# Down-sampled attention: 112 keys by head plus 32 keys by query group in place of 80 and 64

## The chip, the cores and the metric

The kernel runs on one core of a Trainium2 chip, in one launch. The metric is the device time of that core in microseconds. Three runs of the kernel before took 971.51, 972.09 and 972.30 us, a median of 972.09 us.

## What is computed

An attention layer over 8 batches, 8 heads, 576 positions and 64 values per head is followed by a two-layer feed-forward block over 4608 tokens. The attention is the sum of two parts: one on means of four positions, repeated four times, and one in a band of width 7.

```python
q_d, k_d, v_d = (mean over 4 positions of q, k, v)      # 144 positions
out_d = softmax(q_d @ k_d.T / 8) @ v_d
out_up = np.repeat(out_d, 4, axis=2)
mask = np.abs(pos[:, None] - pos[None, :]) < 4
out_local = softmax(where(mask, q @ k.T / 8, -1e9)) @ v
x = (out_up + out_local), heads side by side            # 4608 x 512
h = x @ w_in                                            # 4608 x 2048
out = (s * np.maximum(h, 0) ** 2 + b) @ w_out           # 4608 x 512
```

The change touches the product `softmax(...) @ v_d` alone.

## The kernel before

**Feed-forward.** Tokens are cut into 18 tiles of 256 (t), the 2048 hidden columns into 8 parts of 256 (p). A step (t, p) is `gemm1` (24 matmuls `ph`, lines 556 to 558, 256 columns each) and, two or three steps later, `gemm2` (12 matmuls `po`, lines 601 to 603, 512 columns each). Each operand is split into a high and a low part in a reduced format, which is why every product stands there three times.

**Attention.** A pair is one batch and two heads; there are 32. The first 12 pairs go through `first_unit`, which does the band on TensorE too: `sl` (line 388, scores, in tiles of 64 rows by 32 columns of the array) and `ol` (line 431, 128 rows by 64 columns, so that a matmul of one head writes the upper 64 output partitions and that of the other head the lower). The other 20 pairs go through `two_pairs`, two at a time: `down_unit` for each of the two pairs, and beside it `local_unit`, which does the band on VectorE and GpSimd (`pr`, `st`, `pv`, `acc`, lines 466 to 488).

**The down-sampled part, `down`.** All 32 pairs go through it. Two query groups of both heads lie in one matrix: `qc` is block diagonal, so that one matmul `sa` (line 303) gives for query group i (48 queries, 3 groups) the scores of both heads in 96 output partitions, with 144 key columns. The exponentials `pd` are scaled on ScalarE (line 314). Then they have to be transposed, since the next product sums over keys. The 144 keys are cut in KM = 80 and KR = 64:

- three transposes `tp` (lines 322, 325) put the first 80 keys of each query group in 80 partitions, and three `tr` (line 327) the last 64 keys in 64 partitions;
- ScalarE copies `tp` to `ptm` (line 329) and `tr` to `ptr` (line 332), the two heads' 64 keys one above the other;
- GpSimd adds the four positions of each value: lines 287 and 288 make two partial sums `vt`, `vq` out of the loaded `tvd`, `tvr`, and lines 291 and 292 write them into `vm` (each head's 64 columns, zeros in the other 64) and into the block-diagonal `vdr`;
- `up` (lines 337, 339) is then three matmuls that all use the whole array: 128 rows by 128 columns for the 64 keys of both heads, and twice 80 rows by 128 columns, once for each head. In the trace a float32 matmul is two records, so `up` is six of them, `sa` six, and a transpose one.

`vm` and `vdr` lie in a constant tile `dq` for all pairs but three, so GpSimd writes them for the next pair only when `up` of this one is done.

**What orders the work.** The program is recorded in the order of the step loop, and `advance` draws so many pieces of attention per step from a generator by numbers of due steps. Then a scheduler orders each engine's queue by a simulation of its own, with priorities: `first(b)` gives `sa`, `tp`, `tr` and `up` of batches 3 to 7 a high one, so that they stand wherever the simulation has them ready, also between two `ph` or `po`. Every engine then runs its queue strictly in that order. All loads go through SyncE's one queue (SP).

## Time and profile before

| what | value |
|---|---|
| median of 3 runs | 972.09 us |
| the profiled execution itself | 972.49 us |
| its span | 970.7 us |
| TensorE (PE) busy | 938.7 us, 97% of the span |
| TensorE weight loads (PEld) | 843.4 us, 87% |
| VectorE (DVE) busy | 637.7 us, 66% |
| ScalarE (ACT) busy | 475.0 us, 49% |
| GpSimd (POOL) busy | 418.0 us, 43% |

The span is the time from the first to the last recorded instruction; 1.8 us of the execution lie around it. In the timeline a row has the start, the duration, engine, line, operation, output and inputs, then rows by columns of the weights, the result's shape, and the count of merged records. Matmuls are pipelined: a row's duration runs from the entry of the first column to the exit of the last, so that rows overlap, and the price of a matmul in a stream is the distance from its start to the next start, not its duration.

### The profile page before, as it was taken

Reading aid. Unit: us, or ns where it says so; the run is one execution under the profiler, and the core shown is the slowest. Engines: PE = TensorE matmul, PEld = TensorE weight load, DVE = VectorE, ACT = ScalarE, POOL = GpSimd, SP = SyncE. Lnnn points to the kernel's source line nnn. Section 1 sums busy time; section 2 is a strip of 40 time slices with the busy share of each in tenths; the row PEclk is TensorE's granted clock in tenths of the full one; section 3 lists DMA queues with packets and bytes.
Section 4 is the critical chain, followed back from the end, with each engine's and each line's share of the span. In section 5 each row is a group of like instructions: output and inputs, shape, how many; then the busy total and the mean of one; then the engine's idle time right before and its main releaser. Section 6 shows DMA issues by size and latency. Waiting matters only on the chain.

```text
span 970.7 us, 18541 instructions
## 1 busy us (share of the span) xinstructions
PE 938.7 (97%) x7316; PEld 843.4 (87%) x7316; DVE 637.7 (66%) x1175; ACT 475.0 (49%) x1141; POOL 418.0 (43%) x455
## 2 busy tenths in 40 slices
PE   5769999999999999999999999999999999999998
PEld 4559988888999999998888899989899999998987
DVE  5999996864567878787787878787878521211121
ACT  5878775553754453545363545453635433333231
POOL 9421011101066686776868786867676200000000
PEclk9999999999999999999999999999999999999999
DMA  9736512112243232323241424242412000000000
GB/s 316 261 121 210 172 60 78 49 42 73 101 134 113 77 110 72 102 70 133 67 136 66 135 68 131 72 134 69 136 55 76 1 22 1 23 1 22 1 23 22
DMA packets 32103, 86.26 MB, mean 89 GB/s; under 512 B 3344, under 2 KB 7952, under 8 KB 32016
## 3 DMA queue, kind: packets, MB, share of 16 engines
q1 hardware_dynamic: 32016, 85.08, 26.6%
q8 instruction: 57, 0.93, 0.4%
q14 instruction: 30, 0.25, 0.1%
HBM read 75.63 MB, written 9.44 MB: 88 GB/s over the span
## 4 chain that ended last, share of the span: by engine, by line
PE 74%; DVE 9%; DMA 8%; POOL 5%; ACT 2%; issue 2%; SPq 0%; DVEq 0%; ACTq 0%; POOLq 0%
PE ph L556 11%; PE ph L557 11%; PE ph L558 11%; PE po L603 11%; PE po L601 11%; PE po L602 11%; DMA tqk<-in_qk_dram 3%; POOL pr L466 3%; POOL acc L488 3%; DMA wst<-in_moe_w_out_dram 2%; PE sa L303 2%; DVE bias L579 1%; PE up L339 1%; PE ol L431 1%; DMA lqk<-in_qkn_dram 1%
## 5 line engine op out<-in xcount | busy, mean ns | idle before, releaser
L556 PE MATMUL ph<-xh,wi 128*128 128x256 f32 x1152 | 325.4, 283 | 3.7 <-ACT xh L542 2.5
L557 PE MATMUL ph<-xl,wi 128*128 128x256 f32 x1152 | 323.9, 281 | 0.0
L558 PE MATMUL ph<-xh,wi 128*128 128x256 f32 x1152 | 323.6, 281 | 0.0
L466 POOL TENSOR_TENSOR pr<-lqk 128x576 f32<-128x576 f32 x140 | 201.2, 1461 | 73.2 <-DMA lqk<-in_qkn_dram 29.2
L556 PEld LDWEIGHTS ph<-xh,wi 128*128 128x128 f32 x1152 | 217.5, 189 | 11.2 <-ACT xh L542 2.8
L557 PEld LDWEIGHTS ph<-xl,wi 128*128 128x128 f32 x1152 | 217.4, 189 | 5.4 <-issue 0.2
L558 PEld LDWEIGHTS ph<-xh,wi 128*128 128x128 f32 x1152 | 217.6, 189 | 0.3
L566 ACT ACTIVATE ph<-ph 128x512 f32<-128x512 f32 x144 | 83.8, 582 | 229.0 <-PE ph L558 223.2
L601 PE MATMUL po<-wo,gh 128*128 128x512 f32 x456 | 180.7, 396 | 0.0
L602 PE MATMUL po<-wo,gh 128*128 128x512 f32 x456 | 180.5, 396 | 0.0
L603 PE MATMUL po<-wo,gl 128*128 128x512 f32 x456 | 177.9, 397 | 0.0
L569 DVE TENSOR_TENSOR gl<-ph,gh 128x512 fp32r<-128x512 f32 x114 | 77.8, 683 | 115.8 <-ACT gh L568 115.5
L488 POOL TENSOR_TENSOR acc<-acc,pv 128x576 f32<-128x576 f32 x80 | 114.4, 1430 | 57.1 <-DVE acc L488 29.5
L468 DVE TENSOR_REDUCE st<-pr 128x9 f32<-128x576 f32 x140 | 105.9, 757 | 37.7 <-POOL pr L466 35.4
L292 POOL TENSOR_TENSOR dq<-vq 64x64 f32<-64x64 f32 x58 | 22.8, 393 | 197.4 <-PE up L337 195.3
L603 PEld LDWEIGHTS po<-wo,gl 128*128 128x128 f32 x456 | 85.7, 188 | 17.6 <-issue 0.2
L487 DVE TENSOR_TENSOR pv<-lv,st 128x576 f32<-128x576 f32 x120 | 87.5, 747 | 18.8 <-POOL acc L488 18.4
L601 PEld LDWEIGHTS po<-wo,gh 128*128 128x128 f32 x456 | 85.7, 188 | 15.9 <-ACT gh L568 0.6
L602 PEld LDWEIGHTS po<-wo,gh 128*128 128x128 f32 x456 | 85.7, 188 | 15.8
L568 ACT CAST gh<-ph 128x512 fp32r<-128x512 f32 x114 | 66.9, 587 | 64.3 <-PE po L602 62.4
L567 ACT ACTIVATE ph<-ph 128x512 f32<-128x512 f32 x144 | 83.7, 582 | 3.2
L602 PE MATMUL po<-wo,gb 128*128 128x512 f32 x120 | 47.1, 392 | 0.0
(149 smaller groups left out, 1239.3 us busy)
## 6 DMA issues: line engine op xcount, KB each, us to landing
tqk<-in_qk_dram SPq DMA_DIRECT2D x30, 584.0 KB, 4.1
lqk<-in_qkn_dram SPq DMA_DIRECT2D x20, 768.0 KB, 4.2
lv<-in_vn_dram SPq DMA_DIRECT2D x20, 480.0 KB, 3.4
out_dram<-os SPq DMA_DIRECT2D x17, 512.0 KB, 3.1
wst<-in_moe_w_in_dram SPq DMA_DIRECT2D x7, 1024.0 KB, 6.5
wst<-in_moe_w_out_dram SPq DMA_DIRECT2D x7, 1024.0 KB, 5.3
tvd<-in_vdm_dram SPq DMA_DIRECT2D x29, 160.0 KB, 2.9
tvr<-in_vr_dram SPq DMA_DIRECT2D x29, 128.0 KB, 3.1
```

What stands on the lines that cost most here:

```text
L466: nc.gpsimd.tensor_tensor(pr, lqk[:, 0:CH], lqk[:, CH + o : 2 * CH + o], ALU.mult)
L468: nc.vector.tensor_reduce(ls[:, :, o], pr, AX.X, ALU.add)
L487: nc.vector.tensor_tensor(pv, lv[:, o : o + CH], w, ALU.mult)
L488: (nc.vector if o % 3 == 1 else nc.gpsimd).tensor_tensor(acc[:, :, h], acc[:, :, h], pv, ALU.add)
L556: nc.tensor.matmul(ph[:, j], wi[p][:, 0, k, f], xh[:, k], start=(k == 0), stop=False)
L557: nc.tensor.matmul(ph[:, j], wi[p][:, 0, k, f], xl[:, k], start=False, stop=False)
L558: nc.tensor.matmul(ph[:, j], wi[p][:, 1, k, f], xh[:, k], start=False, stop=(k == NK - 1))
L566: nc.scalar.activation(ph, ph, AF.Relu)
L567: nc.scalar.activation(ph, ph, AF.Square)
L601: nc.tensor.matmul(po[m], gh[:, j, ms], wo[p][:, 0, j], start=first, stop=False)
L602: nc.tensor.matmul(po[m], gh[:, j, ms], wo[p][:, 1, j], start=False, stop=False)
L603: nc.tensor.matmul(po[m], gl[:, j, ms], wo[p][:, 0, j], start=False, stop=last)
```

## The change

KM goes from 80 to 112 and KR from 64 to 32.

- **Last keys.** The last 32 keys of the three query groups are no longer scaled in place: VectorE writes them, scaled, side by side in a tile `rest` (96 queries by 3 times 32 keys). One transpose `tr` puts them in 96 partitions, 32 for each query group. Three copies instead of two put them in `ptr`, which is block diagonal over query groups and zero elsewhere (it took the room of `vdr` and `vm` in `dq`). The values of the last 32 keys are loaded three times, one below the other.
- **First keys.** Three transposes `tp` have 112 key columns instead of 80.
- **Sums of values.** Two additions each for `tvd` and `tvr`, in place, in the tile that the DMA filled. `vt`, `vq`, `vm` and `vdr` are gone, and the matmuls read `tvd` and `tvr` themselves.
- **`up`.** Four matmuls instead of three. Each is 64 columns wide and writes the 64 output partitions of one head: two with 112 rows (`tvd`, `ptm`), then two with 96 rows (`tvr`, `ptr`).
- Loads grow by 64 KB each for `tvd` and `tvr`, per pair.

```diff
-KM = 80
+KM = 112
 KR = SD - KM
+NR = NQ * KR
...
-        vt = tmp([P, 2, P], "vt")
-        vq = tmp([P, 2, D], "vq")
-        ve = nc.gpsimd
-        ve.tensor_tensor(vt[0:KM], tvd[:, 0:2], tvd[:, 2:4], ALU.add)
-        ve.tensor_tensor(vq, tvr[:, 0:2], tvr[:, 2:4], ALU.add)
-        for h in range(2):
-            hs = slice(64 * h, 64 * h + 64)
-            ve.tensor_tensor(vm[:, h, hs], vt[0:KM, 0, hs], vt[0:KM, 1, hs], ALU.add)
-            ve.tensor_tensor(vdr[hs, hs], vq[hs, 0], vq[hs, 1], ALU.add)
+        for v in (tvd, tvr):
+            nc.gpsimd.tensor_tensor(v[:, 0:2], v[:, 0:2], v[:, 2:4], ALU.add)
+            nc.gpsimd.tensor_tensor(v[:, 0], v[:, 0], v[:, 1], ALU.add)
...
+        rest = tmp([P, NQ, KR], "rest")[0:n]
+        nc.vector.tensor_tensor(
+            rest, pd[:, :, KM:SD], dsm.unsqueeze(2).to_broadcast([n, NQ, KR]), ALU.mult)
         for i in range(NQ):
-            nc.scalar.mul(pd[:, i], pd[:, i], dsm[:, i : i + 1])
+            nc.scalar.mul(pd[:, i, 0:KM], pd[:, i, 0:KM], dsm[:, i : i + 1])
...
-                for i in range(NQ):
-                    nc.tensor.transpose(tr[:, i], pd[:, i, KM:SD], ident[0:n, 0:n])
+                nc.tensor.transpose(
+                    tr.rearrange("p h q -> p (h q)"), rest.rearrange("p i k -> p (i k)"),
+                    ident[0:n, 0:n])
...
-        for h in range(2):
-            nc.scalar.copy(ptr[64 * h : 64 * h + 64], tr[:, :, GQ * h : GQ * h + GQ])
+        for i in range(NQ):
+            ks = slice(KR * i, KR * i + KR)
+            nc.scalar.copy(ptr[ks, :, GQ * i : GQ * i + GQ], tr[ks])
...
-            nc.tensor.matmul(up, vdr, ptr.rearrange("p i s -> p (i s)"), start=True, stop=False)
-            for h in range(2):
+            for h, hs in heads:
                 nc.tensor.matmul(
-                    up.rearrange("p (i s) -> p i s", i=NQ), vm[:, h],
-                    ptm[:, :, GQ * h : GQ * h + GQ], start=False, stop=h == 1)
+                    up[hs].rearrange("p (i s) -> p i s", i=NQ), tvd[:, 0, hs],
+                    ptm[:, :, GQ * h : GQ * h + GQ], start=True, stop=False)
+            for h, hs in heads:
+                nc.tensor.matmul(up[hs], tvr[:, 0, hs], ptr[:, h], start=False, stop=True)
```

The first place is TensorE's queue where `up` of a group's first pair meets `sa` of its second. Before:

```order
L601 MATMUL po_7805<-wo_1991,gh_8085 128x512
L303 MATMUL sa_8852<-kd_8780,dq_139 96x144 x2
L337 MATMUL up_8774<-ptr_8750,dq_139 128x144
L339 MATMUL up_8774<-ptm_8748,dq_139 128x144
L303 MATMUL sa_8852<-kd_8780,dq_139 96x144
L339 MATMUL up_8774<-ptm_8748,dq_139 128x144
L602 MATMUL po_7805<-wo_1991,gh_8085 128x512
```

The same place in the changed kernel, whose `up` is lines 338 and 342, whose `sa` is line 297 and whose feed-forward lines are one higher:

```order
L604 MATMUL po_8329<-wo_700,gl_8084 128x512
L338 MATMUL up_8692<-ptm_8666,tvd_8411 64x144
L297 MATMUL sa_8767<-kd_8699,dq_139 96x144
L338 MATMUL up_8692<-ptm_8666,tvd_8411 64x144
L297 MATMUL sa_8767<-kd_8699,dq_139 96x144
L342 MATMUL up_8692<-dq_139,tvr_8409 64x144
L297 MATMUL sa_8767<-kd_8699,dq_139 96x144
L342 MATMUL up_8692<-dq_139,tvr_8409 64x144
L602 MATMUL po_8329<-wo_700,gh_8083 128x512
```

The three full-width matmuls of `up`, which stood among those of `sa`, became four half-width ones that alternate with them one by one.

The second place is TensorE's queue in an earlier pair of the changed kernel, where `up` (lines 338 and 342) stands in `ph`:

```order
L558 MATMUL ph<-xl,wi 128x256
L338 MATMUL up<-ptm,tvd 64x144 x2
L559 MATMUL ph<-xh,wi 128x256
L342 MATMUL up<-dq,tvr 64x144 x2
L557 MATMUL ph<-xh,wi 128x256
```

Here the four are in two lots with a `ph` between. Over the 28 pairs whose `up` comes after the first `ph`, the queue of the changed kernel has the four together in 10 pairs, in two lots of two in 8, and one by one in 10. The scheduler also cut other work otherwise: from the first `ph` on, the lots of `sl` and `ol` that stand between full-array matmuls are 29 in the queue before and 37 now, since one `sl` of a late `first_unit` was dealt out one matmul at a time between `ph`.

The third place is the SP queue, in a group late in the program. Before:

```order
L114 DMA tvr_7929<-in_vr_dram 128x256
L114 DMA tvd_7931<-in_vdm_dram 80x512
L461 DMA lv_7322<-in_vn_dram 128x960
L459 DMA lqk_7645<-in_qkn_dram 128x1536
L114 DMA tqk_7927<-in_qk_dram 128x1168
L461 DMA lv_7647<-in_vn_dram 128x960
```

The same place in the changed kernel (`tvd_7250` is read by the second pair of this group, `tvd_7859` by the first of the next):

```order
L460 DMA lqk_7572<-in_qkn_dram 128x1536
L115 DMA tqk_7855<-in_qk_dram 128x1168
L616 DMA out_0_dram<-os_7112 128x2x512
L115 DMA tvd_7250<-in_vdm_dram 112x512
L115 DMA tvr_7248<-in_vr_dram 96x512
L115 DMA tqk_7861<-in_qk_dram 128x1168
L462 DMA lv_7574<-in_vn_dram 128x960
L115 DMA tvd_7859<-in_vdm_dram 112x512
L115 DMA tvr_7857<-in_vr_dram 96x512
L460 DMA lqk_7869<-in_qkn_dram 128x1536
```

The loads of `tvd` and `tvr` were ahead of a group's other loads, and now stand behind the `up` that reads the tile's former content, with `lv` or `lqk` of the band behind them in the queue.

More of the change, by code (lines that the diff above doesn't have):

```diff
@@ L117, in load_pair @@
         tqk = load("qk", [P, 2, SP], qk[b, hp], two)
-        tvr = load("vr", [P, FAC, D], vr_in[b, hp])
+        tvr = load("vr", [NR, FAC, P], vr_in[b, hp])
         tvd = load("vd", [KM, FAC, P], vdm[b, hp])
@@ L174, in attention_ffn_kernel, with blocks @@
     nc.vector.memset(db, 0.0)
[L176 to L181 removed]
+    def blocks(qc, ptr):
+        return take(qc, 0, [P, NQ, 2 * GQ]), take(ptr, 0, [NR, 2, SD])
+    diag = {0: (db, *blocks(dq[:, 0:QC], dq[:, QC:]))}
     def clear(i):
[L184 to L189 removed]
+        da, n = room[i]["dg"], 2 * NG * P
+        ptr = room[i]["sc"][:, 1248:1536]
+        for j in range(0, n + QC, 456):
+            nc.gpsimd.memset(da[:, j : min(j + 456, n + QC)], 0.0)
+        nc.gpsimd.memset(ptr, 0.0)
+        diag[i] = (take(da, 0, [P, 2 * NG, P]), *blocks(da[:, n : n + QC], ptr))
     wi, wo, wst = {}, {}, {}
@@ L268, in down @@
     def down(b, hp, banks, tmp, dg):
-        _, qc, vdr, vm = dg
+        _, qc, ptr = dg
         tqk, _, tvr, tvd = ld[(b, hp)]
@@ L355, in tmp @@
                 return one.tile(shape, F32, tag=name, name=name)
-            if name in ("ups", "ptr"):
-                spots[name] = spots["qd" if name == "ups" else "kd"]
+            if name in ("ups", "ptm"):
+                spots[name] = spots["qd"]
             else:
@@ L407, in first_unit @@
         if own:
-            pt = take(sc, spots["vt"], [P, 2 * NG, 32])
+            pt = tmp([P, 2 * NG, 32], "pt")
         else:
```

23 lines of the change are left out of this document (7 added, 16 removed).

## The prediction

> **What bounds the kernel now.** I read the page's busy times first, then the windows, then the waits, then TensorE's timeline at the places that the change touches. The page, and three stretches of the windows (start and end, length, then busy time of each engine with its instructions, granted clock, DMA share, GB/s):
>
> ```profile
> PE 938.7 (97%) x7316; PEld 843.4 (87%) x7316; DVE 637.7 (66%) x1175; ACT 475.0 (49%) x1141; POOL 418.0 (43%) x455
> ```
>
> ```profile
> 0.00:66.50 66.50, 42.66 (x677) 34.28 (x677) 53.28 (x122) 45.97 (x131) 37.78 (x81) 1.00 0.73 244
> 66.50:275.00 208.50, 206.18 (x2077) 182.35 (x2078) 154.74 (x296) 130.62 (x304) 23.28 (x43) 1.00 0.31 101
> ...
> 550.00:775.00 225.00, 225.00 (x1519) 206.00 (x1518) 179.00 (x324) 108.46 (x275) 159.05 (x151) 1.00 0.27 88
> ```
>
> After the first 66.5 us TensorE has work without a break: 2.3 us idle in the second stretch, none in the third, while VectorE and GpSimd have 46 and 66 us free there. So from 66.5 us on the time is the sum of what stands in TensorE's queue, and an edit is worth what it takes from or adds to that queue. Ahead of that, TensorE waits; the waits show for what:
>
> ```profile
> POOL dq L292 <- PE up L337: 195.3, 13, 33.3
> ...
> PE sa L303 <- DVE kd L278: 7.3, 1, 7.3
> ```
>
> The last row is the longest wait of TensorE: `sa` of the fifth pair, whose q and k come behind the first weights. GpSimd's 195.3 us are waits for `up` before it may write `dq`; nobody on TensorE waits for them.
>
> **The price of `up` and of the transposes.** One `up` between two `ph`:
>
> ```profile
> 760.00 0.28 PE L556 MATMUL ph<-xh,wi 128*128 128x256 f32 x1
> 760.11 0.41 PE L337 MATMUL up<-ptr,dq 128*128 128x144 f32 x2
> 760.36 0.66 PE L339 MATMUL up<-ptm,dq 80*128 80x144 f32 x4
> 760.75 0.38 PE L557 MATMUL ph<-xl,wi 128*128 128x256 f32 x1
> 760.97 0.28 PE L558 MATMUL ph<-xh,wi 128*128 128x256 f32 x1
> 761.09 0.28 PE L556 MATMUL ph<-xh,wi 128*128 128x256 f32 x1
> ```
>
> A `ph` takes 0.12 us (760.97 to 761.09). From 760.00 to 760.97 there are two of them and the six records of `up`: 0.97 - 0.24 = 0.73 us, 0.122 for each pass of 144 columns. The transposes between two `po`:
>
> ```profile
> 756.00 0.25 PE L322 MATMUL tp<-ident,pd 96*80 96x96 f32 x1
> 756.09 0.33 PE L325 MATMUL tp<-ident,pd 96*80 96x96 f32 x2
> 756.25 0.41 PE L327 MATMUL tr<-ident,pd 96*64 96x96 f32 x3
> 756.44 0.48 PE L602 MATMUL po<-wo,gh 128*128 128x512 f32 x1
> 756.76 0.39 PE L603 MATMUL po<-wo,gl 128*128 128x512 f32 x1
> 757.00 0.39 PE L601 MATMUL po<-wo,gh 128*128 128x512 f32 x1
> ```
>
> A `po` takes 0.24, so the six take 756.00 to 756.76 less 0.24, 0.52 us or 0.087 each. `tp` loads 80 columns and `tr` 64, and they take the same: the 96 columns that stream through set the time.
>
> **What half-width matmuls cost.** This trace has them: `ol`, 64 columns wide, one head to the upper and one to the lower output partitions, as the new `up`. Twenty-four records in a row, and twelve:
>
> ```profile
> 268.45 0.28 PE L558 MATMUL ph<-xh,wi 128*128 128x256 f32 x1
> 268.66 1.21 PE L431 MATMUL ol<-db,tvw 128*64 128x96 f32 x24
> 269.80 0.38 PE L556 MATMUL ph<-xh,wi 128*128 128x256 f32 x1
> 270.02 0.28 PE L557 MATMUL ph<-xl,wi 128*128 128x256 f32 x1
> ```
>
> ```profile
> 151.94 0.28 PE L556 MATMUL ph<-xh,wi 128*128 128x256 f32 x1
> 152.15 0.72 PE L431 MATMUL ol<-db,tvw 128*64 128x96 f32 x12
> 152.80 0.38 PE L557 MATMUL ph<-xl,wi 128*128 128x256 f32 x1
> 153.02 0.28 PE L558 MATMUL ph<-xh,wi 128*128 128x256 f32 x1
> ```
>
> With two `ph` taken off, 24 cost 1.57 - 0.24 = 1.33 us and 12 cost 1.08 - 0.24 = 0.84. Twelve more cost 0.49, 0.082 for two, where one full-width pass of 96 columns cost 0.087: the two halves do run side by side. But 0.84 - 0.49 = 0.35 us is left, whatever the number: the price of going into the narrow shape and out again. The smallest lot confirms it, two records of 32 columns in the 64 by 32 shape between single `ph`:
>
> ```profile
> 172.42 0.24 PE L388 MATMUL sl<-tqk 64*32 64x32 f32 x2
> 172.59 0.38 PE L557 MATMUL ph<-xl,wi 128*128 128x256 f32 x1
> 172.91 0.24 PE L388 MATMUL sl<-tqk 64*32 64x32 f32 x2
> ```
>
> One turn takes 0.49; less 0.12 for `ph` and 2 x 0.087/3 = 0.06 for 32 columns twice, 0.31 us stay. Alternating full-width matmuls costs nothing of the kind: `sa` and `up`, mixed,
>
> ```profile
> 694.46 0.65 PE L303 MATMUL sa<-kd,dq 128*96 128x144 f32 x4
> 694.95 0.41 PE L337 MATMUL up<-ptr,dq 128*128 128x144 f32 x2
> ...
> 695.45 0.41 PE L303 MATMUL sa<-kd,dq 128*96 128x144 f32 x2
> ...
> 696.18 0.40 PE L603 MATMUL po<-wo,gl 128*128 128x512 f32 x1
> ```
>
> take 1.72 - 0.24 = 1.48 us for twelve passes, 0.123 each. I take 0.33 us for each lot, with 0.31 and 0.35 as ends.
>
> [...]
>
> **The sum on TensorE**, for the 28 pairs whose `up` comes after the first `ph`, by the lots in the changed queue:
>
> - Four together, 10 pairs: 0.33 + 4 x 0.122 = 0.82 each, 8.2 us.
> - Two lots of two, 8 pairs: each lot holds both heads, 0.33 + 2 x 0.122 = 0.57; 16 lots, 9.1 us.
> - One by one between `sa`, 10 pairs: nothing to share the array with, 0.33 + 2 x 0.122 = 0.57; 40 lots, 22.8 us.
> - Together 40.1 us, for 28 x 0.73 = 20.4 before: +19.7 us.
> - The 37 - 29 = 8 more lots of `sl` and `ol`: 8 x 0.33 = +2.6 us.
> - Transposes, six to four: -2 x 0.087 = -0.17 a pair, -4.8 us. `tp` now loads 112 columns; if loading set the time, 3 x 0.087 x 112/80 + 0.087 x 96/80 = 0.47 for 0.52, -1.4 us. I take -4.8, as 64 and 80 made no difference.
>
> That is +17.5 us. Two rows for the rest:
>
> ```profile
> L287 POOL TENSOR_TENSOR vt<-tvd 80x256 f32<-80x256 f32 x29 | 22.8, 786 | 0.3
> tvd<-in_vdm_dram SPq DMA_DIRECT2D x29, 160.0 KB, 2.9
> ```
>
> **Start.** The first four pairs load 512 KB more ahead of the weights; the fifth pair's `tvr` and `tvd`, 288 KB, move behind its `tqk`. 224 KB at 244 GB/s are 0.9 us on the load that the 7.3 us wait ends with: +1. The five pairs' extra lots fall where TensorE is idle a third of the time. Bounds: -2 (their two transposes and GpSimd's small additions go) to +4 (the lots and their order bind).
>
> **Covered by TensorE's queue.** GpSimd has four additions in place of six, the largest 786 ns as L287's row: no more than before. VectorE gets `rest`, one instruction a pair with 96 numbers a row for the 256 of L287's (an estimate, from another engine's row); ScalarE three short copies for two. All have a fifth or more of their time free after 66.5 us; were that gone, 28 instructions under 0.8 us would be at most 22 us of VectorE. Of the 2.3 us in which TensorE waits now, the longer queue should swallow about 1.
>
> Profiled 972.5 + 17.5 + 1 - 1 = 990.0 us. The profiled execution took 972.49, 0.4 over the median of 972.09, so this stands for the median too.
>
> **Rivals.**
>
> 1. *The lots cost nothing extra*, only the sharing counts. 18 pairs at 0.49 for 0.73 (-4.3), 10 pairs one by one at 0.98 (+2.5), transposes -4.8: 966 us, faster. It decides if a lot costs under 0.08 us. For it is the pairing in `ol`; against it all three rows above. Chance 0.06.
> 2. *One by one between `sa` is cheap*, the price falls once per stretch: 10 x (0.33 + 0.98) = 13.1 for 22.8, 980 us. The `sl` turns at 172 us speak against it. Chance 0.08.
> 3. *`up` doesn't pair*, because the two passes of a head follow each other directly: 0.33 + 0.98 for four, 0.33 + 0.49 for two, 40 x 0.57 one by one, 49.0 for 40.1: 999 us. `ol` stands in the same order of heads and pairs. Chance 0.07.
> 4. *The wait that the change adds.* `tvd` and `tvr` can be loaded only after the `up` of the pair before, SP stands there with `lv` and `lqk` behind it, and GpSimd stands in its own queue until they land (2.9 us, and a little more for the second), with `acc` behind it. `ot` at the end of a group shows the pace:
>
> ```profile
> 676.53 0.98 PE ot L498 x9
> 726.18 0.98 PE ot L498 x9
> ```
>
> 49.65 us a group, to which TensorE's queue now adds 1.55 + 0.09 - 0.34 = 1.3. If GpSimd's chain is as long as TensorE's now and grows by 2.9, it passes it by 1.6 us in 10 groups; half to all of that is 8 to 16 us more, 1002 us. It needs more than 1.3 us of growth. Against it: GpSimd is free 66 of 225 us. Chance 0.12.
>
> The forecast has 0.65. The last 0.02 are for gains and losses that meet near zero.
>
> **Range and chances.** Lots at 0.31 or 0.35 are -1.5 or +1.5 on 74 lots, the transposes up to +3.4, the start -3 to +3: 985 to 998 for the forecast. With rivals 2 and 3 and most of rival 4 inside, 979 to 1004 leaves out rival 1, the near-zero cases and a tail. A difference of 0.2%, 2 us, is about what a measurement of this kernel tells from none. Faster 0.06, within it 0.02, slower 0.92.
>
> **What would show it.** The profile after should have TensorE without a break from about 67 us on; an `up` of four together at about 0.82 us, and one by one with `sa` at about 0.74 + 4 x 0.57 = 3.0 us for 1.48; four transposes at 0.35. I am wrong if those stretches are as short as now, or if TensorE waits for `lv`, `tvd` or `acc` by more than some 4 us after 67 us.

## The result, and the profile after

The changed kernel takes 1006.08 us (median of 4 runs, 1003.33 to 1007.87) beside 971.8 for the kernel before: 1.0353 times as long, 95% interval 1.0326 to 1.038. Slower was right; 990.0 was 16 us too low, and the range ended at 1004. The profiled execution took 1007.87 us, its span is 1006.1. The page's busy times, and the same stretches of the windows:

```profile
PE 965.7 (96%) x7316; PEld 842.6 (84%) x7316; DVE 666.1 (66%) x1207; ACT 476.7 (47%) x1173; POOL 419.1 (42%) x391
```

```profile
66.50:275.00 208.50, 199.25 (x1955) 169.68 (x1954) 152.77 (x292) 120.14 (x282) 22.12 (x28) 0.96 0.31 100
550.00:775.00 225.00, 224.54 (x1458) 197.50 (x1458) 181.05 (x320) 102.89 (x269) 162.27 (x130) 1.00 0.31 96
```

From 550 to 775 us TensorE has next to no break (0.5 us), as forecast. Between 66.5 and 275 us it is idle for 9.3 us (2.3 before), and the granted clock is 0.96. What TensorE waits for in that stretch:

```profile
PE po L602 <- ACT gh L569: 3.8, 3, 2.3
PE sl L384 <- DVE pl L395: 2.5, 1, 2.5
PE sl L384 <- ACT pd L301: 2.2, 1, 2.2
PE ol L432 <- ACT db L415: 0.8, 1, 0.8
```

The clock has to be read with care. The trace of the kernel before has no clock record ahead of 72.6 us, and the windows count a missing record as 1.00; the 1.00 of its first stretch, 0 to 66.5 us, shows nothing. The distance from `ph` to `ph` in that trace shows that it ran at half clock right up to there:

```profile
72.18 0.41 PE L558 MATMUL ph<-xh,wi 128*128 128x256 f32 x1
72.39 0.36 PE L556 MATMUL ph<-xh,wi 128*128 128x256 f32 x1
...
72.83 0.28 PE L556 MATMUL ph<-xh,wi 128*128 128x256 f32 x1
72.95 0.28 PE L557 MATMUL ph<-xl,wi 128*128 128x256 f32 x1
```

0.21 us became 0.12. In the changed kernel `ph` stands 0.21 us apart too where its record has 0.50, up to 67.3 us, and 0.12 behind. The first five `sa` of the kernel before, at 7 to 44 us, take 0.24 us a record as well, for 0.12 behind 72.6. So only what lies behind 72.6 us can be compared. There the kernel before has full clock up to its end. The changed kernel has half clock at 74.1 to 77.5, 173.1 to 179.9, 220.9 to 224.3 and 238.0 to 241.4 us. From 72.6 to 275 us TensorE is idle for 8.1 us (1.8 before), and it is busy for 14.5 us at half clock, of which I count half, 7.3 us, as lost (an estimate, from the recorded 0.50): together some 13.6 us more than before.

**The lots cost what was forecast.** `up` with four passes together between two `ph`, and one by one between `sa`:

```profile
643.49 0.28 PE L559 MATMUL ph<-xh,wi 128*128 128x256 f32 x1
643.70 0.47 PE L338 MATMUL up<-ptm,tvd 112*64 112x144 f32 x4
643.99 0.42 PE L342 MATMUL up<-dq,tvr 96*64 96x144 f32 x4
644.34 0.38 PE L557 MATMUL ph<-xh,wi 128*128 128x256 f32 x1
644.56 0.28 PE L558 MATMUL ph<-xl,wi 128*128 128x256 f32 x1
...
678.93 0.40 PE L604 MATMUL po<-wo,gl 128*128 128x512 f32 x1
679.25 0.46 PE L338 MATMUL up<-ptm,tvd 112*64 112x144 f32 x2
679.64 0.49 PE L297 MATMUL sa<-kd,dq 128*96 128x144 f32 x2
...
681.67 0.46 PE L342 MATMUL up<-dq,tvr 96*64 96x144 f32 x2
682.06 0.50 PE L602 MATMUL po<-wo,gh 128*128 128x512 f32 x1
682.39 0.40 PE L603 MATMUL po<-wo,gh 128*128 128x512 f32 x1
```

643.49 to 644.56 holds two `ph` (0.23) and `up`: 0.84 us, forecast 0.82. 678.93 to 682.39 holds two `po` (0.47) and the mixed stretch: 3.0 us, forecast 3.0; all nine mixed stretches behind 350 us take as long. The transposes:

```profile
586.53 0.25 PE L319 MATMUL tp<-ident,pd 96*112 96x96 f32 x1
586.62 0.33 PE L322 MATMUL tp<-ident,pd 96*112 96x96 f32 x2
586.78 0.25 PE L323 MATMUL tr<-ident,rest 96*96 96x96 f32 x1
586.81 0.48 PE L602 MATMUL po<-wo,gh 128*128 128x512 f32 x1
587.13 0.40 PE L603 MATMUL po<-wo,gh 128*128 128x512 f32 x1
```

587.13 - 586.53 less one `po` is 0.36 us, forecast 0.35: 0.09 each with 112 and 96 columns to load, where 80 and 64 took 0.087.

**Something else is slower: `ph` itself.** The first and the last of the 24 `ph` of one step (t = 15, p = 2), far behind the last attention, before and after:

```profile
839.24 0.28 PE L556 MATMUL ph<-xh,wi 128*128 128x256 f32 x1
...
841.86 0.28 PE L558 MATMUL ph<-xh,wi 128*128 128x256 f32 x1
```

```profile
873.07 0.28 PE L557 MATMUL ph<-xh,wi 128*128 128x256 f32 x1
...
875.82 0.28 PE L559 MATMUL ph<-xh,wi 128*128 128x256 f32 x1
```

23 intervals in 2.62 us (114 ns each) became 2.75 us (119.6). The change does not touch the instructions of `ph`.

**Two stages.** To place a loss I count the 5184 matmuls of `ph` and `po` and take from each trace the start of the 1400th and of the last. The 1400th starts at 331.4 us before and 347.7 after, the last 635.2 us later before and 654.3 after. So 16.3 us are lost in the first stage and 19.1 in the second.

The second stage is what the queue holds: nine mixed stretches at 3.0 for 1.48 us are 13.7 us more, the transposes in it 1.8 us less, and the slower `ph` is 6.4 us (the run with 192 bytes, below). That makes 18.3 of 19.1. In the first stage most of the loss is the idle time and the half clock above.

### The profile page after: what moved, and what is told of

The parts are those of the page before. It is cut to its first block, busy times and chain, and to the rows that moved or that the text cites. A ratio compares the mean times of both kernels' runs of the same rounds, so it can differ in the third digit from the quotient of the medians.

```text
span 1006.1 us, 18578 instructions
## 1 busy us (share of the span) xinstructions
PE 965.7 (96%) x7316; PEld 842.6 (84%) x7316; DVE 666.1 (66%) x1207; ACT 476.7 (47%) x1173; POOL 419.1 (42%) x391
## 4 chain that ended last, share of the span: by engine, by line
PE 81%; DVE 8%; DMA 3%; ACT 3%; POOL 3%; issue 2%; SPq 0%; DVEq 0%; ACTq 0%; POOLq 0%
PE ph L557 13%; PE ph L559 12%; PE ph L558 12%; PE po L602 12%; PE po L603 12%; PE po L604 12%; PE sa L297 2%; DMA tqk<-in_qk_dram 2%; POOL pr L467 2%; PE up L338 1%; PE up L342 1%; POOL acc L489 1%; PE sl L389 1%; PE ol L432 1%; PE ot L499 1%
## 5 line engine op out<-in xcount | busy, mean ns | idle before, releaser
L557 PE MATMUL ph<-xh,wi 128*128 128x256 f32 x1152 | 329.7, 286 | 2.8 <-ACT xh L543 1.4
L559 PE MATMUL ph<-xh,wi 128*128 128x256 f32 x1152 | 326.7, 284 | 0.0
L467 POOL TENSOR_TENSOR pr<-lqk 128x576 f32<-128x576 f32 x140 | 204.3, 1484 | 78.8 <-DMA lqk<-in_qkn_dram 53.3
L557 PEld LDWEIGHTS ph<-xh,wi 128*128 128x128 f32 x1152 | 219.8, 191 | 13.6 <-DVE gl L570 3.1
L558 PEld LDWEIGHTS ph<-xl,wi 128*128 128x128 f32 x1152 | 220.1, 191 | 6.0 <-issue 0.8
L559 PEld LDWEIGHTS ph<-xh,wi 128*128 128x128 f32 x1152 | 219.9, 191 | 1.6 <-issue 1.2
L489 POOL TENSOR_TENSOR acc<-acc,pv 128x576 f32<-128x576 f32 x80 | 116.6, 1457 | 56.8 <-DVE acc L489 40.9
L285 POOL TENSOR_TENSOR tvd<-tvd 112x256 f32<-112x256 f32 x29 | 25.3, 872 | 231.4 <-DMA tvd<-in_vdm_dram 158.2
```

Of the source, the lines that this page charges most:

```text
L467: nc.gpsimd.tensor_tensor(pr, lqk[:, 0:CH], lqk[:, CH + o : 2 * CH + o], ALU.mult)
L489: (nc.vector if o % 3 == 1 else nc.gpsimd).tensor_tensor(acc[:, :, h], acc[:, :, h], pv, ALU.add)
L557: nc.tensor.matmul(ph[:, j], wi[p][:, 0, k, f], xh[:, k], start=(k == 0), stop=False)
L558: nc.tensor.matmul(ph[:, j], wi[p][:, 0, k, f], xl[:, k], start=False, stop=False)
L559: nc.tensor.matmul(ph[:, j], wi[p][:, 1, k, f], xh[:, k], start=False, stop=(k == NK - 1))
```

## The experiments

Each time is a median, and each ratio is to runs of the kernel before on the same chip, with its 95% interval. "First" and "second" are the two stages of the profiled execution.

### Where xh and xl lie

The change makes some tiles smaller and others larger, so everything behind them moves in SBUF. Distances below are from `wi` to `xh` (the same to `xl`) in bytes of one partition. In the kernel before they are 960 for parts 2 to 6 and 320 for parts 0, 1 and 7 (modulo 2048), in the changed kernel 1280 and 320. They follow from the sizes of the tiles; a trace shows no addresses.

```diff
-    split_w(0)
+    gap = one.tile([P, 48], F32, tag="gap", name="gap"); split_w(0)
```

> The changed kernel with 192 unused bytes per partition ahead of wi for parts 0, 1 and 7; every instruction and its order as in the changed kernel. Theory A (the pace of ph is set by how far xh and xl lie from wi in SBUF): the distance for parts 2 to 6 goes from 1280 to 1472 (modulo 2048), which is 192 modulo 256 as it was in the kernel before (960): ph of parts 2 to 6 from 119.7 back to 113.5 ns an interval, 5/8 of 3456 x 6 ns = 12 to 13 us less, 993 to 995 us. Parts 0, 1 and 7 stay at 117.8. Theory B (ph is slower because of what runs beside it, or of the clock): no change, 1006 us.

Measured: 999.89 us, 1.0281 (1.0263 to 1.0299); first 345.4, second 647.9. The same step as above:

```profile
866.00 0.28 PE L557 MATMUL ph<-xh,wi 128*128 128x256 f32 x1
...
868.62 0.28 PE L559 MATMUL ph<-xh,wi 128*128 128x256 f32 x1
```

2.62 us, as in the kernel before. Then the opposite, in the kernel before:

```diff
-    two = ctx.enter_context(tc.tile_pool(name="two", bufs=2))
+    mid = ctx.enter_context(tc.tile_pool(name="mid", bufs=1)); two = ctx.enter_context(tc.tile_pool(name="two", bufs=2))
...
-    sb_s = cst.tile([P, 1], F32, name="sb_s")
+    sb_s = mid.tile([P, 1], F32, name="sb_s")
...
-    sb_b = cst.tile([P, 1], F32, name="sb_b")
+    sb_b = mid.tile([P, 1], F32, name="sb_b")
```

> The kernel before with the two one-number tiles sb_s and sb_b moved behind the weights, so that all of wi lies 64 bytes lower and xh, xl stay; instructions and order as before. Theory A (distance): parts 2 to 6 from 960 to 1024 modulo 2048, the residue 0 modulo 256 that t = 2 has now, 113.5 to 119.7 ns; parts 0, 1 and 7 from 320 to 384, 117.8 to between 118 and 120: +13 to +15 us, 985 to 987 us, without any other part of the change. Theory B (the pace comes from what runs beside): 972 us.

Measured: 979.64 us, 1.0074 (1.0058 to 1.009); first 332.2, second 641.3.

```profile
844.05 0.28 PE L556 MATMUL ph<-xh,wi 128*128 128x256 f32 x1
...
846.80 0.28 PE L558 MATMUL ph<-xh,wi 128*128 128x256 f32 x1
```

Theory A holds both ways, and TensorE's queue has the same order in each pair of kernels; theory B falls. The first edit moves `xh` and `xl` and leaves `wi` of parts 2 to 6 where it was, the second moves `wi` alone: so the pace goes with the distance, not with one operand's place. The size was expected nearly twice as large as it came, because parts 2 to 6 of the kernel before do not run at 113.5 ns throughout: they change between 113.5 and 117.8 from step to step; the mean is 115.3 (here and below, over the intervals from `ph` to `ph` under 130 ns, token tiles from t = 3 on). Behind the 1400th matmul the mean from `ph` to `ph` is 117.9 ns before and 121.1 here, 3.2 x 2372 = 7.6 us.

Last, parts 0, 1 and 7 of the kernel before (`mid` is made as above):

```diff
-                return one.tile(shape, F32, tag=name, name=name)
+                return (mid if name == "ptm" else one).tile(shape, F32, tag=name, name=name)
...
-        lambda shape, name: one.tile(shape, F32, tag=name, name=name),
+        lambda shape, name: (mid if name == "ptm" else one).tile(shape, F32, tag=name, name=name),
```

> The kernel before with ptm's tile moved from ahead of wi for parts 0, 1 and 7 to behind all weights: their distance to xh and xl goes from 320 to 1472 modulo 2048, 192 modulo 256 as parts 2 to 6 have. Theory A (distance): ph of parts 0, 1 and 7 from 117.8 to 113.5 ns, 3/8 of 3456 x 4.3 = 5.6 us at most, half of it if they alternate between the two values as parts 2 to 6 do in the local stage: 966.5 to 969.5 us. Theory B: 972.

Measured: 970.7 us, 0.998 (0.9969 to 0.9991), first 329.9, second 632.3. It is the only kernel here that is faster than the kernel before, by 0.2%. The expectation was mostly missed: those parts went from 117.6 to 116.4 ns in the mean, but parts 2 to 6, whose distance did not change, from 115.3 to 116.2. What these runs show is two classes: at the distances 1280, 1024 and 384, multiples of 128, `ph` took 119.4 to 119.6 ns in the mean; at 960, 320 and 1472, 64 beside a multiple, it took 113.5 or 117.8 in a step and 115.0 to 117.7 in the mean. What chooses between these two stays open, and so does whether the rule is one of 128 bytes.

### The lots of up

In the changed kernel, the operand that is ready last goes first, and `sa` of batches 3 to 7 queues behind the `up` before it:

```diff
+                mm = nc.tensor.matmul(up[hs], tvr[:, 0, hs], ptr[:, h], start=True, stop=False)
...
+                mm = nc.tensor.matmul(
+                    up[hs].rearrange("p (i s) -> p i s", i=NQ), tvd[:, 0, hs],
+                    ptm[:, :, GQ * h : GQ * h + GQ], start=False, stop=True)
+        ups_last[0] = mm
...
+        prev = ups_last[0]
-        with first(b):
+        with first(b), tc.issue_after(getattr(prev, "ins", prev)) if b >= 3 else contextlib.nullcontext():
```

> The changed kernel with the four passes of up always together: tvr with ptr is added first (its operand is ready last), and sa queues behind the up before it. Theory A (each change of shape on TensorE has its price, and only the lots count): 10 stretches with sa from 3.00 to 1.55 us (0.74 + 0.82), -14.5; 8 pairs with two lots from 1.29 to 0.84, -3.6: 988 us. Rival (the time shows up elsewhere: TensorE waits for acc, lv or tvd as long as it was busy with lots): above 1000 us. ph keeps 119.7 ns in parts 2 to 6.

Measured: 1000.71 us, 1.0282 (1.026 to 1.0305); first 346.8, second 651.5. The busy time of TensorE falls by 17 us, to 948.3, and only 5 to 7 us of it arrive: the rival. TensorE now waits in the second stage, 10.2 us from 275 to 800 (2.0 in the changed kernel), the longest first:

```profile
PE ph L560 <- DVE gl L573: 4.0, 4, 1.4
PE po L605 <- ACT gh L572: 2.5, 2, 2.2
PE po L605 <- DVE os L617: 1.0, 2, 0.6
PE tr L325 <- DVE rest L310: 1.0, 2, 0.5
```

No lots for `up` at all:

```diff
-            nc.gpsimd.tensor_tensor(v[:, 0], v[:, 0], v[:, 1], ALU.add)
+            for h in range(2):
+                hs, no = slice(64 * h, 64 * h + 64), slice(64 - 64 * h, 128 - 64 * h)
+                nc.gpsimd.tensor_tensor(v[:, 2 + h, hs], v[:, 0, hs], v[:, 1, hs], ALU.add)
+                nc.gpsimd.memset(v[:, 2 + h, no], 0.0)
...
+                nc.tensor.matmul(up, tvr[:, 2 + h], ptr[:, h], start=h == 0, stop=False)
...
+                    up.rearrange("p (i s) -> p i s", i=NQ), tvd[:, 2 + h],
```

> The changed kernel with up in full columns again: GpSimd puts each head's sums into a slice whose other half it sets to zero, so four passes of 128x128 and no lot for up. Keys stay 112 and 32, four transposes. Theory A (lots): 28 pairs at 4 x 0.122 = 0.49 us against 40.1 us in all as forecast, -26.4 us: 979 to 980 us; what is left over the kernel before is the pace of ph (+12), less the transposes (-4.8). If the stalls and the low clock before 275 us come of the lots of sl and ol too, they go as well: 970 to 972. Rival (GpSimd, with ten short instructions a pair for four, holds up the groups): over 990 us.

Measured: 1001.96 us, 1.0314 (1.0285 to 1.0343); first 349.7, second 645.6. The expectation fails, and the first stage, with no lot of `up` in it, is as long as ever. So taking the lots out is not enough to win it back. This edit also gives GpSimd ten short instructions a pair for four and makes another order, and what these cost was not measured.

And the lots alone, in the kernel before:

```diff
-            nc.tensor.matmul(up, vdr, ptr.rearrange("p i s -> p (i s)"), start=True, stop=False)
...
+            heads = [(h, slice(64 * h, 64 * h + 64)) for h in range(2)]
+            for h, hs in heads:
+                nc.tensor.matmul(
+                    up[hs].rearrange("p (i s) -> p i s", i=NQ), vm[:, h, hs],
+                    ptm[:, :, GQ * h : GQ * h + GQ], start=True, stop=False)
+            for h, hs in heads:
+                nc.tensor.matmul(
+                    up[hs], vdr[:, hs], ptr.rearrange("p i s -> p (i s)"), start=False, stop=True)
```

> The kernel before with up alone in half columns: four passes of 64 columns, one head each, the first keys' pair ahead of the last keys' pair; keys stay 80 and 64, sums, transposes and tiles as before. In TensorE's queue ten pairs have their four passes one by one between sa. Theory A (lots): the ten stretches 1.52 us longer, +15; the other pairs 0.09 each or 0.45 where they are two lots, +2 to +3: 989 us, nearly all of it after the 1400th matmul, ph at the pace of before. Rival (the price needs the changed kernel's other parts): under 980.

Measured: 989.37 us, 1.0181 (1.0164 to 1.0198); first 336.7 (+5.3), second 645.8 (+10.6). Theory A has the total to the microsecond, but it expected nearly all of it behind the 1400th matmul, and a third lies ahead of it. Then together:

```diff
+            for h, hs in heads:
+                mm = nc.tensor.matmul(
+                    up[hs], vdr[:, hs], ptr.rearrange("p i s -> p (i s)"), start=True, stop=False)
...
+        with first(b), tc.issue_after(getattr(prev, "ins", prev)) if b >= 3 else contextlib.nullcontext():
```

> As the run before it, but the four passes always together (the last keys' pair first, sa queued behind the up before). Theory A: 28 lots at 0.33 us with four passes of 0.122 for 0.73 us: +2.5 us in all, later stage +1 to +2. The order in the first stage has the two heads' sl back to back, as in the changed kernel: Theory E adds 3 to 6 us there: 975 to 981 us. If the local chain suffers as it did in the changed kernel with up together (sa behind up): later stage +8 or more, over 982.

Measured: 977.77 us, 1.0058 (1.0043 to 1.0073); first 335.8 (+4.4), second 633.9 (-1.2). Keeping the narrow passes together takes back 11.6 us, the whole loss of the second stage. Here the local chain does not suffer, as it did with the same edit in the changed kernel. So that kernel has something that hinders the chain.

### VectorE's rest

```profile
371.04 1.43 POOL L489 TENSOR_TENSOR acc<-acc,pv 128x576 f32<-128x576 f32 x1
371.65 4.53 DVE L308 TENSOR_TENSOR rest<-pd,dsm 96x96 f32<-96x96 f32 x1
372.43 0.46 POOL L286 TENSOR_TENSOR tvd<-tvd 112x128 f32<-112x128 f32 x1
372.84 0.45 POOL L286 TENSOR_TENSOR tvr<-tvr 96x128 f32<-96x128 f32 x1
373.26 2.81 POOL L467 TENSOR_TENSOR pr<-lqk 128x576 f32<-128x576 f32 x2
```

That is the timeline of the changed kernel, VectorE and GpSimd. All 29 `rest` in small tiles, with shortest, median and longest ns and the first and last start:

```profile
L308 DVE TENSOR_TENSOR rest<-pd,dsm x29: 245/255/4532, 14.0 to 787.7; 96x96 f32<-96x96 f32 x29
```

Of the 29, 17 took 245 to 257 ns, 16 of them with GpSimd idle but for 0.03 us at most and one, at 14.0 us, 255 ns with GpSimd busy all along. The other 12 took 566 to 4532 ns, with GpSimd busy for about nine tenths of that or more. The longest starts at 371.65 and ends at 376.18, 0.11 us after the fifth GpSimd instruction, each of which had begun before the one ahead of it ended. What VectorE has queued behind `rest` waits with it: `gb` starts at 376.11. In the run with up together, `ph` waits for `gl` and `gb` for 4.4 us. So VectorE stood while five GpSimd instructions ran in a row; what makes it stand is not shown.

On top of the run with up together, ScalarE writes `rest`:

```diff
-        nc.vector.tensor_tensor(
-            rest, pd[:, :, KM:SD], dsm.unsqueeze(2).to_broadcast([n, NQ, KR]), ALU.mult)
+            nc.scalar.mul(rest[:, i], pd[:, i, KM:SD], dsm[:, i : i + 1])
```

> As the run with up together, but ScalarE writes rest (three short multiplications) in place of VectorE's one. In the changed kernel's trace VectorE's instruction for rest took 247 ns where GpSimd was idle and 566 to 4532 ns where GpSimd ran one instruction after another (29 of them 26.7 us). Theory C (VectorE held up by GpSimd makes gl, and so ph, late, which the run with up together shows as 4.4 us of waits for gl and gb, 1.0 for rest): these waits go, 993 to 996 us for 1000.7. Rival D (the local chain is held by the SP queue, which waits for up): no change, 999 to 1001 us, groups of local attention still 54 to 55 us apart.

Measured: 988.71 us, 1.018 (1.0152 to 1.0207): 1.0 points under the run before it. First 339.2, second 642.6, so 7.6 and 8.9 us less (the profiled execution of the run before it took 1004.28 us, 3.6 above its median). Theory C, and more than it had expected.

The other theory, that SP's wait for `up` holds the chain:

```diff
-        for v in (tvd, tvr):
+        vs = [x[:, 0] if b == 0 and hp else tmp([x.shape[0], P], nm) for x, nm in ((tvd, "vsd"), (tvr, "vsr"))]
+        for v, s in zip((tvd, tvr), vs):
...
-            nc.gpsimd.tensor_tensor(v[:, 0], v[:, 0], v[:, 1], ALU.add)
+            nc.gpsimd.tensor_tensor(s, v[:, 0], v[:, 1], ALU.add)
...
```

> As the run with up together, but the last additions of the down-sampled values go to two small tiles of their own (outside of the first batch), so that tvd and tvr can be loaded again as soon as GpSimd has read them, and not after up. Rival D (SP stands at these loads until up is done, 66 us of 400 between 400 and 800 us, with lqk and lv behind it, and GpSimd waits 55 us for lqk against 19 before): SP's waits for up go, groups of local attention from 54.7 to 52 us or less, 990 to 994 us for 1000.7. Theory C (VectorE behind GpSimd): 999 to 1001.

Measured: 995.7 us, 1.0252 (1.0229 to 1.0276), 0.3 points less, with overlapping intervals; first 342.3, second 646.6. SP's waits for `up` are gone, though it waits 32 us for GpSimd's sums instead, and groups are 50 to 54 us apart. The time lies between the two expectations: D holds a small part at most. Both edits together:

> Both edits on top of the run with up together. If C and D each hold a part: TensorE is the bound again in the local stage, groups 50 to 51 us apart, 985 to 989 us: what stays over 972 is then the pace of ph (+6 to +8), lots (28 at 0.33 for up, +8.7 for sl and ol at most), the early stalls and the half clock behind them, less transposes. If neither: 999 to 1001.

Measured: 991.77 us, 1.0189 (1.0163 to 1.0214), first 341.9, second 644.5: no less than with `rest` on ScalarE alone, and above the 985 to 989 expected. So D shows no further gain once C is mended.

The same edit in the changed kernel alone, `up` as it was:

> The changed kernel with one edit: ScalarE writes rest (three short multiplications) in place of VectorE's one; up as in the changed kernel. Theory C1 (in the changed kernel TensorE is the bound after 275 us, it waits 2 us there, so rest costs little): 1002 to 1005 us. Theory C2 (VectorE's hold-ups are part of the 16 us by which the changed kernel is slower than forecast): 994 to 999 us.

Measured: 1002.8 us, 1.0308 (1.0289 to 1.0327); first 341.2 (-6.5), second 655.3 (+1.0). That is 4 us by the ratios, as C1 says: in the second stage nothing is gained. C1's reason, that TensorE has lots to do while VectorE stands, fits the waits of 2.0 us there. The gain lies in the first stage.

Now an instruction of this kind alone. The kernel before gets one, with a result that nobody reads:

```diff
         nc.vector.reciprocal(dsm, dsm)
+        nc.vector.tensor_tensor(
+            take(vq.rearrange("p a c -> p (a c)")[0:n], 0, [n, NQ, 32]), pd[:, :, 48:KM],
+            dsm.unsqueeze(2).to_broadcast([n, NQ, 32]), ALU.mult)
```

> The kernel before with one more VectorE instruction a pair, of the shape of rest (96 numbers a row from pd and dsm), written where nobody reads it; nothing else. With it the two heads' sl of the fourth pair of the second batch stand back to back on TensorE, as in the changed kernel. Counted by where the 1400th of the 5184 matmuls of ph and po starts (331.4 us in the kernel before, 635.1 from there to the last): Theory F (VectorE's extra instruction and the order it brings cost time in the first stage, where VectorE is busy 9 tenths, with waits and half clock): first stage +5 to +10, later +0 to +3, 978 to 984 us. Rival (a quarter of a microsecond on VectorE is nothing): 972 to 974.

Measured: 991.88 us, 1.0207 (1.0191 to 1.0222): 19.7 us for one instruction a pair. First 345.2 (+13.8), second 640.7 (+5.6). Theory F, and twice its size. But the edit brings more than an instruction: it writes into `vq`, which GpSimd needs for the next pair's sums, and GpSimd now waits for it (total, times, longest):

```profile
POOL vq L288 <- DVE vq L313: 114.9, 16, 29.5
```

In the changed kernel GpSimd waits nowhere for `rest`. So the 19.7 us are those of the instruction, the order that it brings and this tie to GpSimd together. Two runs take it apart in part. Only the pairs of batches 3 to 7 get it:

```diff
+        if (b, hp) not in units[:EU]:
+            nc.vector.tensor_tensor(
```

> The kernel before with VectorE's extra instruction only in the pairs of the last ten groups (one head pair after another beside the local attention), none in the first three batches; TensorE's order is that of the kernel before up to the 1089th matmul of ph and po. With the instruction in all pairs it was +13.8 us up to the 1400th and +5.6 behind it. Theory G (the first part comes from the order that the instruction brings there): first stage +0 to +2, later +5 to +7, 977 to 980 us. Rival (the first part comes back later, whatever is done in it): 985 or more.

Measured: 977.27 us, 1.0048 (1.0031 to 1.0066); first 330.2 (-1.2), second 639.3 (+4.1): theory G. TensorE's order is that of the kernel before up to the 1089th matmul, so what is lost in the first stage comes of the instructions there. And all pairs, with 3 numbers a row:

```diff
+        nc.vector.tensor_tensor(vq[0:n, 0, 0:3], pd[:, 0, 48:51], dsm, ALU.mult)
```

> The kernel before with VectorE's extra instruction in all pairs, but with 3 numbers a row in place of 96; the order that it brings has the two heads' sl of the fourth pair of the second batch back to back too. Theory G (order): first stage +8 to +14. [...] Later stage: +5 if what costs there is that VectorE stands until GpSimd has a gap, whatever the size; +0 to +1 if it is the instruction's own time. G with the hold-up: 985 to 992 us; H: 972 to 979.

Measured: 981.6 us, 1.0085 (1.0054 to 1.0115); first 337.3 (+5.9), second 640.6 (+5.5): between the two expectations, 985 to 992 us if the order costs the time of the first stage (G) and 972 to 979 if VectorE's own time does (H). The instruction in the groups of lines, with 96 numbers a row and with 3 (busy, mean ns):

```profile
L313 DVE TENSOR_TENSOR vq<-pd,dsm 96x96 f32<-96x96 f32 x29 | 24.5, 845 | 1.6 <-POOL dq L292 1.0
```

```profile
L313 DVE TENSOR_TENSOR vq<-pd,dsm 96x3 f32<-96x3 f32 x29 | 28.3, 974 | 2.2 <-POOL dq L292 1.3
```

3 numbers take no less time than 96, and the second stage loses the same 5.5 us. So what costs there is not the instruction's own work; that VectorE stands until GpSimd has a gap fits both rows. A rival stays: SP's loads of `tvr` and `tvd` wait longer for GpSimd's sums there (114 us between 400 and 800 us in the run with the late pairs alone, 24 before). In the first stage, where GpSimd is busy for 29.67 of the 208.5 us from 66.5 to 275 and the short one takes 0.15 us (its first three, 151 ns in the mean), 5.9 us are still lost. That is more than its own time; the order or the tie through `vq` (102 us of GpSimd's waits from 66.5 to 330 us) must bring it, and no run parts the two. The long instruction loses 8 us more there, in an order that differs from the short one's. The windows of the two show how (TensorE's busy time first, the clock third from the end), first the long one:

```profile
66.50:275.00 208.50, 198.63 (x1972) 173.83 (x1973) 150.31 (x294) 119.92 (x278) 29.44 (x41) 0.96 0.29 97
```

```profile
66.50:275.00 208.50, 203.31 (x2025) 177.64 (x2025) 150.41 (x298) 126.01 (x289) 29.67 (x44) 1.00 0.28 92
```

TensorE is idle for 9.9 us with the long instruction and 5.2 with the short one, and the clock is 0.96 and 1.00. Behind 72 us the long one has half clock from 159.7 to 163.1 and from 187.0 to 193.9 us, the short one none, as the kernel before. Ahead of that the short one's trace has no clock record either, and its first five `sa` take 0.24 us a record, as those of the kernel before.

### The first stage

What the waits look like there, from TensorE's timeline of the run with the long instruction, at the fourth pair of the second batch:

```profile
175.07 0.26 PE L386 MATMUL sl<-maskb,idb 128*128 128x192 bf16 x1
175.26 0.62 PE L391 MATMUL sl<-tqk 64*32 64x32 f32 x48
176.73 0.26 PE L386 MATMUL sl<-maskb,idb 128*128 128x192 bf16 x1 [0.85 <-DVE pl L397]
...
178.50 0.50 PE L604 MATMUL po<-wo,gh 128*128 128x512 f32 x1 [0.95 <-ACT gh L571]
188.34 0.79 PE L604 MATMUL po<-wo,gh 128*128 128x512 f32 x1 [3.37 <-ACT gh L571]
```

The second head's `sl` follows the first at once and waits for VectorE; in the kernel before eight `po` stood between them. The wait there is no longer than in the kernel before (0.85 us for 1.06); the one that counts is the 3.37 us for `gh` from 185 us on, in which the half clock of 187.0 to 193.9 us begins. The scheduler orders by its own simulation, and one more instruction on VectorE moves all that comes after. In the changed kernel the place of the two `sl` costs 2.2 and 2.5 us of waiting, and the clock behind it:

```profile
165.00:170.00 5.00, 5.00 (x36) 4.58 (x36) 3.19 (x8) 2.15 (x5) 0.00 (x0) 1.00 0.38 131
170.00:175.00 5.00, 1.41 (x54) 0.99 (x52) 3.10 (x10) 3.23 (x13) 0.00 (x0) 0.81 0.18 52
175.00:180.00 5.00, 3.93 (x58) 3.31 (x59) 3.80 (x12) 2.66 (x7) 0.00 (x0) 0.51 0.51 161
180.00:185.00 5.00, 5.00 (x35) 4.42 (x34) 4.05 (x10) 2.90 (x7) 0.00 (x0) 1.00 0.04 14
```

TensorE is busy for 1.41 of 5 us, and from 173.1 to 179.9 us the clock is half. A wait of 2.2 us ended at 172.7, and half clock began at 173.1, ahead of the second wait; one of 2.3 us ended at 220.7, and half clock began at 220.9. Of the other two stretches, the one from 74.1 us began 1.9 us behind a wait of 1.1 us and within one of 0.8, and the one from 238.0 us began 7.2 us behind the last wait, one of 0.36 us. So what sets half clock off is not shown. I tried to mend the place of the two `sl` alone in the changed kernel, by queueing the second `sl` behind four `po` of the third block:

```diff
+                if (t, p, m, j) == (2, 0, 1, 0):
+                    mark["po"] = mm
...
+            mm = mark.pop("po", None) if h else None
+            behind = tc.issue_after(getattr(mm, "ins", mm)) if mm else contextlib.nullcontext()
```

> The changed kernel with one edit: at the fourth pair of the second batch the second head's sl queues behind four po of the third block on TensorE, so that the two heads' sl no longer stand back to back (at 172.7 and 176.1 us in the changed kernel, with a wait of 2.5 us for VectorE between them and the granted clock at 0.51 for the 5 us behind it). Theory E (a wait of TensorE costs its length and then half-clock time): 2.5 + 2.5 us go, 1000 to 1003 us, and the clock from 175 to 180 us is above 0.9. Rival (the wait is hidden or comes back at the next pair): 1005 to 1007.

Measured: 1004.42 us, 1.0328 (1.031 to 1.0347), 2.4 us by the ratios and inside the intervals; first 344.2, second 654.3. The clock from 175 to 180 us was 0.50. The wait went elsewhere, one of 3.4 us for `gh` at 171 us, with half clock from 171.0 to 181.3: theory E is not shown by this run, and that the order of the two `sl` costs the time isn't either.

Last, the mended pieces together. Up together, `rest` on ScalarE and the gap:

> The run with up together and rest on ScalarE (988.7 us), with 192 unused bytes ahead of wi for parts 0, 1 and 7. If the pace of ph adds up with the rest: 6 to 8 us less, 981 to 983 us; if the local chain has become the bound instead: 986 to 989.

Measured: 984.64 us, 1.012 (1.0099 to 1.014), 0.6 points under the run without the gap, between the two expectations; first 342.2, second 638.7. And full columns with the same two edits:

> up in full columns (no lot for up), rest on ScalarE, 192 unused bytes: all three costs taken away, while keys stay 112 and 32 with four transposes, and values' sums stay in the tiles that they are loaded in. Against the run before it, 28 times 0.842 - 0.49 = 0.35 us less on TensorE, 9.8 us: 972 to 974 us if TensorE is the bound; 981 or more if SP, which waits for up before it loads again, or GpSimd holds the groups.

Measured: 993.33 us, 1.0213 (1.0192 to 1.0234); first 349.2, second 637.5. The second stage is within 2.5 us of the kernel before. The first is 17.8 us longer, with no lot of `up`, no `rest` on VectorE and `wi` back at the distance class of the kernel before: from 66.5 to 275 us TensorE is idle for 10.9 us there, and the clock is half from 169.0 to 179.2 and 182.6 to 186.0 us. The expectation of 972 to 974 fails on it.

## Why the prediction was wrong

The sum had +17.5 us; the measurement has +34.3. The terms for lots and transposes came out right. What it lacks are two losses that it put at nothing: the pace of `ph`, about 7 us, and the waits and half clock of the first stage, about 13.6 us. They are a little more than the 16.8 us that are missing; an earlier start of the feed-forward gives some back.

- **Lots: right.** 0.84 for 0.82, 3.0 for 3.0. Half columns alone cost the kernel before 17.2 us, where the sum had 19.7 for `up` in an order with more lots of two. Rivals 1, 2 and 3 fall: rival 1 wanted 0.49 for four together, rival 3 1.31, and rival 2 a mixed stretch of about 2.
- **Transposes: right.** 0.36 for 0.35.
- **"From 66.5 us on the time is the sum of what stands in TensorE's queue": failed for the first stage, and took the pace of `ph` as given.** Moving tiles made `ph` slower: 7.0 us come back with the gap in the changed kernel, by the ratios, and a move of 64 bytes costs the kernel before 7.6 us, there in all parts. In the second stage the queue, at that pace, does make up the time. In the first it does not: the waits and the half clock behind them are not in the queue. The row "0.00:66.50" with its clock of 1.00 hid that TensorE ran at half clock there in the kernel before too.
- **"The longer queue should swallow about 1": the wrong sign.** Idle time from 66.5 to 275 us went from 2.3 to 9.3 us. What brings these waits was not isolated.
- **"Covered by TensorE's queue": failed.** I priced `rest` by its length, under 0.8 us, and put it beside other work. It took up to 4.53 us. On ScalarE instead it gives the changed kernel 4 us by the ratios, in the first stage alone, and about 10 us where `up` stands together. A like instruction costs the kernel before 19.7 us, but that figure holds the tie through `vq` and another order too.
- **Start:** the 24th matmul starts 5.5 us earlier than before, not 1 later, outside the bounds of -2 to +4. But 24 `ol` that stood ahead of it stand behind it now, and at the 1400th nothing of the lead is left.
- **Rival 4** came near in time (1002) for another reason. SP does wait for `up` (72 us between 400 and 800), but TensorE waited only 2 us after 275 us. With `up` together, 0.3 points went with SP's wait, and none once `rest` was mended.
- **What would show it:** TensorE should have had no break from 67 us on, and that line named the failure: 9.3 us before 275. The waits were mostly for `gh`, `pl` and `pd`, not for `lv`, `tvd` or `acc`, which the sign named.

Still open: why the first stage is 8 to 18 us longer in every kernel with 112 and 32 keys, with and without `rest` on VectorE. The traces show waits of a few microseconds and half clock behind them, at places that change with the order. Which of the edits brings which order was not separated, and an edit of one place in the order did not win the time back. The single effects do not add up either: 17.2, 7.6 and 19.7 us less 4.8 make 39.7 for 34.3.

## What to carry to other kernels

Do not price an added instruction by its length alone. It can be held up by another engine (`rest` took up to 4.53 us for 245 ns), tie two engines through a tile, and change the order where a scheduler makes the queues: read the order of both kernels around the waits of the bound engine. Keep passes of another array shape together, which gave 11.6 us back here; the operand that is ready last goes first. Before reading a clock of 1.00, look where its record begins. When a change resizes tiles, look at where the operands of the main matmul come to lie, and shift them with a few unused bytes if the pace changes: 192 gave 7.0 us back here.

## What the runs showed of the hardware

- The pace of a 256-column matmul went with the distance in SBUF between its weights and its moving operand: 119.4 to 119.6 ns in the mean at three distances that are multiples of 128 bytes, 113.5 or 117.8 a step at three that lie 64 beside one.
- Going from the whole array to half columns and back cost 0.35 us at `ol`, by the times of 12 records (0.84 us) and 24 (1.33); to the 64 by 32 shape and back 0.31 us, an estimate from a turn of 0.49 us with two records of `sl`; `up` as four half-width passes took 0.84 us between two `ph`, and 1.5 us more than before where the passes stood one by one among `sa`.
- `rest` on VectorE (96 numbers a row, from `pd` and `dsm`), which takes 245 ns alone, stood for up to 4.53 us while GpSimd ran one instruction after another; a like instruction in the kernel before took 845 ns in the mean with 96 numbers a row and 974 with 3.
- In the changed kernel a wait of 2.2 us was followed within 0.5 us by half clock, which lasted 6.8 us with another wait of 2.5 us in it; one of 2.3 us was followed by half clock for 3.4 us. Half clock from 238.0 to 241.4 us had no wait over 0.36 us in the 17 us ahead of it, and a wait of 1.06 us in the kernel before was followed by none.
- The kernel before too ran at half clock ahead of 72.6 us: `ph` 0.21 us apart for 0.12, its first five `sa` 0.24 us a record for 0.12, where the profile has no clock record and prints 1.00.
